# Uneven pieces of the first modulation's last block: 800 columns in six transfers in place of 480

## The chip, the cores and the metric

The kernel runs on one core of one Trainium2 chip. The metric is the device time of one execution in microseconds (us); of several runs the median is given. A profile is one execution with the hardware profiler, and its span goes from the first to the last instruction of the program.

## The reference

One token goes through an adaLN block with a cached attention and a dense layer. Cut to what matters:

```python
mod = silu(c) @ w_mod                        # c: 640, w_mod: 640 x 3840
sa, ca, ga, sb, cb, gb = six parts of 640
h = layernorm(x) * (1 + ca) + sa             # first modulation: sa, ca
q = (h @ wq)  -> 32 heads of 192
p = softmax(q . k_cache * 192**-0.5)         # k_cache, v_cache: 32 x 8192 x 192
x = x + ga * ((p . v_cache) @ wo)
h = layernorm(x) * (1 + cb) + sb
x = x + gb * (relu(h @ w1 + b1)**2 @ w2 + b2)
```

All of it is float32, and the two caches are 403 MB of the 452 MB that are read.

## The kernel before

Everything comes through one queue of transfers that SyncE (SP) issues in the order in which the code says `load`. The caches, with the slices of `wq` and `wo` that are due, lie in memory as "chunks" of 128 rows (one for each partition) of up to `SLOT` = 16128 columns. `PLAN` (from `plan`, L56) says which key positions and value units a chunk holds. Three buffers of that size (`slot`, L103) are used in turn: the weights of the first modulation take the first (`wm0_t`), chunks 0 and 1 the next two, and from there `load(n + 3)` (L435) waits until the reader of the buffer is done. After the last chunk the same queue brings the weights of the other modulations, `wm1`, and of the dense layer, `w1` and `w2`, in cuts (`WM_CUT`, `W1_CUT`, `W2_CUT`), the last of which are small: 1920, 1280 and 640 columns.

For each chunk VectorE (DVE) multiplies the keys with the query (L280) and sums over the 192 columns (L288), ScalarE (ACT) takes the exponential (L315), and TensorE (PE) multiplies the probabilities with the values (L332). The program's order on each engine is the order of the code.

The part that the change touches is the start. `mod(0, 2, wm0_t, wm0x_t)` (L252, function at L191) computes `sa` and `ca`: 640 inputs are 5 blocks of 128 (`KB` = 5), and 1280 outputs are 4 groups of 32 rows of PSUM with 2 x 160 columns each. So a block is 4 matmuls of 320 columns, with the block's `silu(c)` as the stationary operand (column b of `e`). Of the last block not all columns are loaded as a full row of each partition. The columns of `wx` (width `WX`) lie apart, in `wm0x`: the piece of each of the 128 rows goes to some partition below 64 and to one of `SX` slots there, as the table `XP` says. An entry (a, k, n) of `XP` is one transfer: k rows, at partitions a, a + 4, a + 8 and so on, with n slots each.

```python
SX = 7
XP = ((32, 8, 5), (0, 3, SX), (1, 3, SX), (2, 3, SX), (3, 3, 6), (33, 1, SX))
WX = 3 * DG
```

Here 8 x 5 + 9 x 7 + 3 x 6 + 7 = 128 pieces of 480 columns. The value of `c` that belongs to a piece lies at the same partition and slot in the columns `KB + s` of `e`, zero elsewhere, and the area of the pieces is set to zero before the transfers (L121 on DVE, L122 on GpSimd, POOL), since unused places are multiplied too. L126 issues the six transfers, right behind the main one (L123) and ahead of chunk 0 (L250). In `mod`, L205 multiplies what came as full rows, and L211 the pieces, slot by slot; it waits for all six transfers. Then come the layernorm (L158), the query of the first 512 columns (L261) and the first multiplication of keys (L280).

At the end, L475 multiplies by `w2` block by block as its cuts land, DVE makes `y` (L478, L479), and two small transfers write it out.

Of the kernel before, what the change touches and what calls it, by code (L numbers as in the profile page):

```python
# [13 lines left out]
P = 128  # L14
D = 640
# [5 lines left out]
DG = D // G  # L21
FG = FF // G
KB = DG // 32
# [13 lines left out]
UNIT = E * DH  # L37
EXTRA = {"o": WO, "q": WQ}
SLOT = 84 * DH
SX = 7  # L40
XP = ((32, 8, 5), (0, 3, SX), (1, 3, SX), (2, 3, SX), (3, 3, 6), (33, 1, SX))
WX = 3 * DG
W0 = KB * 2 * D - WX
VPC = 5
LEAD_FROM = 1300
# [41 lines left out]
def width(chunk):  # L87
    return chunk[1] * DH + chunk[3] * UNIT + sum(EXTRA[t] for t, _ in chunk[4])
# [6 lines left out]
def block_kernel(ctx: ExitStack, tc: tile.TileContext, kv, wm0, wm0x, wm1, w1, w2, out):  # L95
    nc = tc.nc
# [6 lines left out]
    def slot(name):  # L103
        return strm.tile([P, SLOT], F32, tag="slot", name=name, bufs=3)


    ident = const.tile([P, P], F32, name="ident")
    make_identity(nc, ident)
    ones = const.tile([P, P], F32, name="ones")
# [6 lines left out]
    eps_t = const.tile([P, 1], F32, name="eps_t")  # L116
    nc.gpsimd.memset(eps_t, EPS)

    wm0_t = slot("wm0_t")
    wm0x_t = wm0_t[:64, SLOT - SX * WX:]  # L120
    nc.vector.memset(wm0x_t[:, :SX // 2 * WX], 0.0)  # L121
    nc.gpsimd.memset(wm0x_t[:, SX // 2 * WX:], 0.0)  # L122
    nc.sync.dma_start(wm0_t[:, :wm0.shape[1]], wm0)  # L123
    r = 0
    for a, k, n in XP:
        nc.sync.dma_start(wm0x_t[a:a + 4 * k - 3:4, :n * WX], wm0x[r:r + k, :n * WX])  # L126
        r += k

    small = const.tile([P, 2 * KB + SX + FB + KB], F32, name="small")
    nc.vector.tensor_copy(small, wm0_t[:, W0 + WQ:wm0.shape[1]])  # L130
    x_c, c_c, bbc = small[:, :KB], small[:, KB:2 * KB + SX], small[:, 2 * KB + SX:]

# [58 lines left out]
    def mod(first, n, w, wx=None, between=lambda: None):  # L191

        ps = psum.tile([P, 512], F32, tag="q", name=f"ps_mod{first}", bufs=1)
        for b in range(KB):
            if b == 3:
                between()
            wb = w[:, b * n * D:(b + 1) * n * D]
            if wx is None or b < KB - 1:
                wb = wb.rearrange("p (m n) -> p m n", m=n)
                parts = [(g, slice(0, n * DG), wb[:, :, DG * g:DG * (g + 1)]) for g in range(G)]  # L200
            else:
                wb = wb[:, :n * 3 * DG].rearrange("p (m n) -> p m n", m=n)
                parts = [(g, slice(0, n * DG), wb[:, :, DG * g:DG * (g + 1)]) for g in range(2)] + [(2, slice(0, DG), wb[:, 0, 2 * DG:])]
            for g, at, wg in parts:
                nc.tensor.matmul(ps[32 * g:32 * (g + 1), at], e[:, b:b + 1].to_broadcast([P, 32]), wg,  # L205
                                 start=(b == 0), stop=(b == KB - 1 and (wx is None or g < 2)))
        if wx is not None:
            wx = wx.rearrange("p (s n) -> p s n", s=SX)
            for s in range(SX):
                for g, at, wg in ((2, slice(DG, 2 * DG), wx[:, s, :DG]), (3, slice(0, 2 * DG), wx[:, s, DG:])):  # L210
                    nc.tensor.matmul(ps[32 * g:32 * (g + 1), at], e[:64, KB + s:KB + s + 1].to_broadcast([64, 32]), wg,  # L211
                                     start=False, stop=(s == SX - 1))
        nc.vector.tensor_copy(mods[:, first:first + n], ps[:, :n * DG].rearrange("p (m n) -> p m n", m=n))

    def gate(m, w, steps):

        ps = psum.tile([P, 512], F32, tag="q", name=f"ps_mod{m}", bufs=1)
        b = 0
        for n in steps:
            for b in range(b, b + n):  # L220
                for k in range(2):
                    nc.tensor.matmul(ps[64 * k:64 * (k + 1), :2 * DG], e[:, b:b + 1].to_broadcast([P, 64]),
                                     w[:, b, 2 * DG * k:2 * DG * (k + 1)], start=(b == 0), stop=(b == KB - 1))
            b += 1
            yield
        for g in range(G):
            r = slice(32 * g, 32 * (g + 1))
            nc.scalar.activation(mods[r, m], ps[r, DG * (g % 2):DG * (g % 2 + 1)], AF.Copy)
        yield

    chunk_t = {}
    start = [sum(width(c) for c in PLAN[:n]) * P for n in range(len(PLAN))]
# [17 lines left out]
    load(0)  # L250
    load(1)
    mod(0, 2, wm0_t, wm0x_t)  # L252
    ma = columns(mods[:, 0:2].rearrange("p m n -> p (m n)"), 2 * DG, "ma")
    h1 = layernorm(x_c, 1, lambda: ma[:, KB:, 0], lambda: ma[:, :KB, 0], "ln1")
# [129 lines left out]
    for n, (kp, nk, vp, nv, extra) in enumerate(PLAN):  # L384
# [3 lines left out]
        at = nk * DH + nv * UNIT  # L388
# [15 lines left out]
        m = nk - FOLD * nk // 16 if kp >= FOLD_FROM else nk  # L404
# [39 lines left out]
    turn(NPAIR - 1)  # L444
    attend(*wo_t)
    mod(2, 3, wm1_t[:, KB * D:KB * 4 * D], between=gather)
    x1 = const.tile([P, DG], F32, name="x1")
    nc.vector.tensor_mul(x1, att_t[0][:, :DG], mods[:, 2])
    nc.vector.tensor_add(x1, x1, x_t)

    last = gate(5, gb_t, (2, 1, 2))
# [4 lines left out]
    for b in range(KB):  # L456
        for g in range(G):
            nc.tensor.matmul(pf[32 * g:32 * (g + 1), :FG], hT2[:, b], w1_t[:, b, FG * g:FG * (g + 1)],
                             start=(b == 0), stop=(b == KB - 1))
# [13 lines left out]
    for b in range(FB):  # L473
        for g in range(G):
            nc.tensor.matmul(py[32 * g:32 * (g + 1), :DG], fT[:, b], w2_t[:, b, DG * g:DG * (g + 1)],  # L475
                             start=(b == 0), stop=(b == FB - 1))
# [57 lines left out]
```

## Time and profile before

| | before |
|---|---|
| median of 3 runs | 1052.11 us (1052.1 to 1052.33) |
| the profiled execution | 1052.17 us |
| its span | 1050.1 us |
| DVE busy | 899.4 us (86%) |
| PE busy | 497.1 us (47%) |
| packets of the loads, share of 16 DMA engines' span | 99.4% |
| read from memory | 451.82 MB, 430 GB/s |
| instructions fetched | 16 packets of 16 KB (queue q8) |

A transfer is split into packets, and the packets run on 16 DMA engines that work side by side. A transfer of 128 rows gives 8 packets, one for each row, to each of the 16 engines; one of 8 rows gives one packet to each of 8 engines, and one of 3 rows to 3. A packet of 4 bytes after a transfer's last packet on an engine reports that its part is done. The view of DMA packets can be asked for any stretch, and it counts the packets that begin in it; the share that it prints is their whole duration over 16 times the stretch. In a stretch of 10 ns, which is 160 ns of 16 engines, a share of 788.1% is a single packet of 1.26 us. In longer stretches of equal small packets, the share times 16 is the number of engines that are at work.

### The profile page before, as it was taken

The page shows a single profiled execution, that of the slowest core. Times are in us where ns is not written, and L with a number is a line of the kernel's source. Part 1 is how long each engine was busy: PE and PEld are TensorE (multiplying, and loading weights), DVE is VectorE, ACT ScalarE, POOL GpSimd, SP SyncE. Part 2 cuts the span into 40 slices and gives each one's busy share as a digit, 9 for nine tenths or more (in the row PEclk, how much of TensorE's full clock was granted, in tenths as well). Part 3 has the DMA queues.
Part 4 walks back from the last instruction along what each step waited for, and adds up shares of the span by engine and source line. Part 5 has one row for each costly group of instructions (what it writes and reads, how often), then busy time and mean ns, then how long its engine had stood idle before and what let it go on. Part 6 is the DMA issues. An engine that isn't in the chain of part 4 may idle for free.

```text
span 1050.1 us, 4948 instructions
## 1 busy us (share of the span) xinstructions
PE 497.1 (47%) x2130; PEld 135.7 (13%) x2130; DVE 899.4 (86%) x304; ACT 51.4 (5%) x156; POOL 11.0 (1%) x12
## 2 busy tenths in 40 slices
PE   3253063655452454347354365354546346435287
PEld 1110010111010011012011011011111011001023
DVE  1699999978969989999797997999999987999822
ACT  0100000000000000000000000000000000000001
POOL 1000000000000000000000000000000000000200
PEclk9676586777666676767676577667768767668689
DMA  9999999999999999999999999999999999999998
GB/s 409 428 433 432 433 436 435 441 439 433 430 435 431 430 435 431 435 436 439 432 431 433 437 432 437 433 433 435 436 430 433 433 437 433 433 433 433 425 429 344
DMA packets 9142, 452.12 MB, mean 431 GB/s; under 512 B 1033, under 2 KB 1037, under 8 KB 1421
## 3 DMA queue, kind: packets, MB, share of 16 engines
q1 hardware_dynamic: 9118, 451.83, 99.4%
q8 instruction: 16, 0.26, 0.1%
q14 instruction: 4, 0.03, 0.0%
q10 hardware_dynamic: 4, 0.00, 0.0%
HBM read 451.82 MB, written 0.00 MB: 430 GB/s over the span
## 4 chain that ended last, share of the span: by engine, by line
DVE 51%; DMA 34%; PE 13%; ACT 1%; issue 1%; SPq 0%; DVEq 0%; ACTq 0%
DMA chunk<-in_kv 31%; DVE sc L288 24%; DVE chunk L280 24%; PE ps_o L332 7%; PE ps_q L261 2%; DMA w_t<-in_w 2%; PE att_a L361 1%; DMA wm_t<-in_wm 1%; PE ps_mx L307 1%; DVE os L345 1%; DVE ps_o L342 1%; ACT p L315 1%; DVE nm L309 1%; PE ps_mod L205 1%; DVE mp L305 0%
## 5 line engine op out<-in xcount | busy, mean ns | idle before, releaser
L280 DVE TENSOR_TENSOR chunk<-chunk,qb 128x8064 f32<-128x8064 f32 (+19 forms) x81 | 419.4, 5208 | 53.1 <-DMA chunk<-in_kv 45.9
L288 DVE TENSOR_REDUCE sc<-chunk 128x44 f32<-128x8448 f32 (+16 forms) x56 | 413.7, 7395 | 0.8
L332 PE MATMUL ps_o<-chunk,p 128*32 128x512 f32 x1536 | 295.8, 735 | 34.6 <-DMA chunk<-in_kv 25.5
L307 PE MATMUL ps_mx<-ident,mp 128*128 128x128 f32 x32 | 14.9, 464 | 352.8 <-DVE mp L305 352.8
L332 PEld LDWEIGHTS ps_o<-chunk,p 128*32 128x32 f32 x1536 | 68.0, 131 | 239.1 <-issue 196.7
L361 PE MATMUL att_a<-chunk,oW 128*32 128x512 f32 x96 | 64.7, 829 | 72.1 <-ACT oW L359 72.1
L261 PE MATMUL ps_q<-chunk,ln_h 128*128 128x512 f32 x110 | 65.6, 756 | 17.9 <-DMA chunk<-in_kv 17.8
L307 PEld LDWEIGHTS ps_mx<-ident,mp 128*128 128x128 f32 x32 | 5.7, 179 | 379.7 <-DVE mp L305 351.9
L315 ACT ACTIVATE p<-sc,nm 128x256 f32<-128x256 f32 x32 | 16.2, 508 | 622.9 <-DVE nm L309 622.9
L261 PEld LDWEIGHTS ps_q<-chunk,ln_h 128*128 128x128 f32 x110 | 26.5, 251 | 54.9 <-issue 34.4
L342 DVE TENSOR_TENSOR ps_o<-ps_o,mask 96x1024 f32<-96x1024 f32 (+1 forms) x17 | 19.7, 1156 | 8.9 <-PE ps_o L332 8.9
L361 PEld LDWEIGHTS att_a<-chunk,oW 128*32 128x32 f32 x96 | 12.2, 142 | 108.1 <-ACT oW L359 74.8
L309 DVE TENSOR_REDUCE nm<-ps_mx 128x1 f32<-128x128 f32 x32 | 9.3, 291 | 17.9 <-PE ps_mx L307 17.9
L345 DVE TENSOR_REDUCE os<-ps_o 96x128 f32<-96x1024 f32 (+1 forms) x17 | 19.7, 1158 | 0.6
L347 PE MATMUL ps_o<-ident,os 96*128 96x96 f32 x16 | 5.3, 332 | 29.0 <-DVE os L345 29.0
L409 POOL TENSOR_TENSOR chunk<-chunk 128x1824 f32<-128x1824 f32 (+1 forms) x2 | 7.9, 3940 | 980.6 <-DVE chunk L280 980.6
L320 PE MATMUL ps_sum<-ident,wide 128*128 128x128 f32 x16 | 7.6, 475 | 21.7 <-ACT wide L318 21.7
L205 PE MATMUL ps_mod<-wm_t,silu 128*32 128x480 f32 (+2 forms) x78 | 10.0, 647 | 14.5 <-DVE silu L187 14.5
L351 DVE TENSOR_REDUCE oT<-ps_o 128x3 f32<-128x96 f32 x16 | 4.0, 248 | 13.7 <-PE ps_o L347 13.7
L359 ACT ACTIVATE oW<-oT,r 128x96 f32<-128x96 f32 x16 | 5.9, 372 | 193.8 <-DVE oT L351 193.8
L363 PE MATMUL att_a<-chunk,oW 128*96 128x384 f32 x32 | 14.8, 543 | 0.0
L262 ACT ACTIVATE qb<-ps_q 128x512 f32<-128x512 f32 x12 | 7.2, 597 | 124.9 <-PE ps_q L261 124.9
(80 smaller groups left out, 103.4 us busy)
## 6 DMA issues: line engine op xcount, KB each, us to landing
chunk<-in_kv SPq DMA_DIRECT2D x38, 8064.0 KB, 31.4
chunk<-in_kv SPq DMA_DIRECT2D x11, 8000.0 KB, 33.5
chunk<-in_kv SPq DMA_DIRECT2D x2, 7872.0 KB
chunk<-in_kv SPq DMA_DIRECT2D x1, 6144.0 KB, 22.5
wm_t<-in_wm SPq DMA_DIRECT2D x1, 4480.0 KB
wm_t<-in_wm SPq DMA_DIRECT2D x1, 4257.0 KB, 12.6
chunk<-in_kv SPq DMA_DIRECT2D x1, 3264.0 KB
chunk<-in_kv SPq DMA_DIRECT2D x1, 3072.0 KB
```

Of the source, the lines that this page charges most:

```text
L205: nc.tensor.matmul(ps[32 * g:32 * (g + 1), at], e[:, b:b + 1].to_broadcast([P, 32]), wg, start=(b == 0), stop=(b == KB - 1 and (wx is None ...
L261: nc.tensor.matmul(ps, h1[:, b:b + 1].to_broadcast([P, P]), w[:, b], start=(b == 0), stop=(b == KB - 1))
L280: nc.vector.tensor_mul(pr, pr, q[:, None, :].to_broadcast([P, b - a, DH]))
L288: nc.vector.tensor_reduce(sc[:, a % SRING:a % SRING + b - a], src[:, a - first:b - first], axis=AX.X, op=ALU.add)
L307: nc.tensor.transpose(ps[:, :P], mp.to_broadcast([P, P]), ident)
L309: nc.vector.tensor_reduce(nm, ps[:, :P], axis=AX.X, op=ALU.max, negate=True)
L315: nc.scalar.activation(p, s[:, :, None].to_broadcast([P, NPOS, 32 // E]), AF.Exp, bias=nm, accum_out=sp[:, h % 2:h % 2 + 1])
L332: nc.tensor.matmul(ps_t[h // 2][32 * g:32 * (g + 1), h % 2], p[:, E * j:E * (j + 1)].rearrange("p e r -> p (e r)"), t[:, g], start=(j == 0 ...
L342: nc.vector.tensor_mul(po, po, mask[:n, None, None, :].to_broadcast([n, b - a, ED, E]))
L345: nc.vector.tensor_reduce(os_t[i][:n, a:b], po, axis=AX.X, op=ALU.add)
L361: nc.tensor.matmul(att_a[96:, :512], oW[:, j], w[:, j, :512], start=(first and j == 0), stop=(last and j == NV - 1))
L363: nc.tensor.matmul(att_a[:96, :NV * (D - 512)], oW.rearrange("p j r -> p (j r)"), w[:, :, 512:], start=first, stop=last)
```

## The change

480 of the last block's 1280 columns were pieces; now 800 are. `WX` is 800 columns, there are 5 slots instead of 7, and the table has two transfers of 8 rows with 5 slots, one of 8 rows with 2, two of 3 rows with 5, and one of a single row with 2. The full rows of `wm0` are 8192 columns wide in place of 8514. `mod` takes one matmul fewer from the full rows, and three for each of 5 slots from the pieces in place of two for each of 7. The setting to zero on DVE is moved to the front of the program and takes 3 of the 5 slots; POOL takes 2.

```diff
-SX = 7
-XP = ((32, 8, 5), (0, 3, SX), (1, 3, SX), (2, 3, SX), (3, 3, 6), (33, 1, SX))
-WX = 3 * DG
+SX = 5
+XP = ((32, 8, SX), (33, 8, SX), (34, 8, 2), (0, 3, SX), (1, 3, SX), (2, 1, 2))
+WX = 5 * DG
 W0 = KB * 2 * D - WX
...
+    wm0_t = slot("wm0_t")
+    wm0x_t = wm0_t[:64, SLOT - SX * WX:]
+    nc.vector.memset(wm0x_t[:, :3 * WX], 0.0)
     ident = const.tile([P, P], F32, name="ident")
     make_identity(nc, ident)
...
-    wm0_t = slot("wm0_t")
-    wm0x_t = wm0_t[:64, SLOT - SX * WX:]
-    nc.vector.memset(wm0x_t[:, :SX // 2 * WX], 0.0)
-    nc.gpsimd.memset(wm0x_t[:, SX // 2 * WX:], 0.0)
+    nc.gpsimd.memset(wm0x_t[:, 3 * WX:], 0.0)
     nc.sync.dma_start(wm0_t[:, :wm0.shape[1]], wm0)
...
-                wb = wb[:, :n * 3 * DG].rearrange("p (m n) -> p m n", m=n)
-                parts = [(g, slice(0, n * DG), wb[:, :, DG * g:DG * (g + 1)]) for g in range(2)] + [(2, slice(0, DG), wb[:, 0, 2 * DG:])]
+                wb = wb[:, :n * 2 * DG].rearrange("p (m n) -> p m n", m=n)
+                parts = [(0, slice(0, n * DG), wb[:, :, :DG]), (1, slice(0, DG), wb[:, 0, DG:])]
...
-                for g, at, wg in ((2, slice(DG, 2 * DG), wx[:, s, :DG]), (3, slice(0, 2 * DG), wx[:, s, DG:])):
+                for g, at, wg in ((1, slice(DG, 2 * DG), wx[:, s, :DG]), (2, slice(0, 2 * DG), wx[:, s, DG:3 * DG]),
+                                  (3, slice(0, 2 * DG), wx[:, s, 3 * DG:])):
                     nc.tensor.matmul(ps[32 * g:32 * (g + 1), at], e[:64, KB + s:KB + s + 1].to_broadcast([64, 32]), wg,
                                      start=False, stop=(s == SX - 1))
```

On SP, at the start of the program, the queue of transfers before was this; a row is line, tensor written and read, rows x columns:

```order
L123 DMA wm_t<-in_wm 128x8514
L126 DMA wm_t<-in_wm0x 8x2400
L126 DMA wm_t<-in_wm0x 3x3360 x3
L126 DMA wm_t<-in_wm0x 3x2880
L126 DMA wm_t<-in_wm0x 1x3360
L247 DMA chunk_104<-in_kv 128x12288
```

And with the change it is this:

```order
L123 DMA wm_t<-in_wm 128x8192
L126 DMA wm_t<-in_wm0x 8x4000 x2
L126 DMA wm_t<-in_wm0x 8x1600
L126 DMA wm_t<-in_wm0x 3x4000 x2
L126 DMA wm_t<-in_wm0x 1x1600
L248 DMA chunk_104<-in_kv 128x12288
```

The number of transfers stays seven ahead of chunk 0; the eight-row ones carry 9600 columns a row in place of 2400, and the three-row ones 8000 in place of 12960.

On DVE, at the start, the order before was:

```order
L113 TENSOR_REDUCE mask<-ident 128x8
L115 TENSOR_REDUCE sel<-ident 128x1
L121 MEMSET wm_t 64x1440
L130 COPY small<-wm_t 128x34
L185 TENSOR_SCALAR silu<-silu 128x12
```

And with the change:

```order
L109 MEMSET wm_t 64x2400
L116 TENSOR_REDUCE mask<-ident 128x8
L118 TENSOR_REDUCE sel<-ident 128x1
L130 COPY small<-wm_t 128x32
L185 TENSOR_SCALAR silu<-silu 128x10
```

The setting to zero moved ahead of the two small reductions, and no other instruction of DVE changed its place.

## Rows read from the trace of the kernel before

**Rows 1.** The page: span, busy times, slices of the DMA engines, queues of packets.
```profile
span 1050.1 us, 4948 instructions
...
PE 497.1 (47%) x2130; PEld 135.7 (13%) x2130; DVE 899.4 (86%) x304; ACT 51.4 (5%) x156; POOL 11.0 (1%) x12
...
DMA  9999999999999999999999999999999999999998
...
q1 hardware_dynamic: 9118, 451.83, 99.4%
q8 instruction: 16, 0.26, 0.1%
```

**Rows 2.** Chain that ended last, 0 to 120 us: start us, us, what.
```profile
0.73 12.57 DMA wm_t<-in_wm
...
14.48 5.55 PE ps_mod L205 x36
20.03 3.96 PE ps_mod L211 x21
...
36.38 12.97 DVE chunk L280
```

**Rows 3.** The same chain, 1000 us to the end.
```profile
1026.34 19.43 DMA w_t<-in_w
...
1045.80 0.75 PE ps_y L475 x16
...
1046.58 0.52 PE ps_y L475 x8
```

**Rows 4.** Stretches near the end; the last two columns: DMA share, GB/s.
```profile
1042.00:1042.90 0.90, 0.85 (x26) 0.88 (x30) 0.00 (x0) 0.00 (x0) 0.00 (x0) 1.00 1.02 427
1043.90:1045.00 1.10, 0.74 (x24) 0.68 (x24) 0.00 (x0) 0.00 (x0) 0.00 (x0) 1.00 0.74 305
1045.35:1045.60 0.25, 0.00 (x0) 0.00 (x0) 0.00 (x0) 0.00 (x0) 0.00 (x0) 1.00 0.59 236
1045.70:1045.80 0.10, 0.00 (x0) 0.00 (x0) 0.00 (x0) 0.00 (x0) 0.00 (x0) 1.00 0.52 205
1046.10:1046.20 0.10, 0.10 (x12) 0.10 (x4) 0.00 (x0) 0.00 (x0) 0.00 (x0) 1.00 0.07 25
```

**Rows 5.** DMA packets in 257.685:257.695, 260.060:260.070, 260.925:260.935 us: packets, MB, share.
```profile
q1 hardware_dynamic: 1, 0.06, 1487.5%
...
q8 instruction: 1, 0.02, 549.4%
...
q1 hardware_dynamic: 1, 0.06, 1830.6%
```

**Rows 6.** DMA packets in 12.589:12.597 us, then in 1046.100:1046.110 us.
```profile
q1 hardware_dynamic: 4, 0.02, 578.1%
...
q1 hardware_dynamic: 1, 0.00, 63.8%
```

**Rows 7.** DMA packets of 10 ns at 3.450 us, then at 38.700 us.
```profile
q1 hardware_dynamic: 1, 0.03, 788.1%
...
q1 hardware_dynamic: 1, 0.06, 1475.6%
```

**Rows 8.** Timeline, 0 to 8 us: start us, us, engine, line, instruction.
```profile
1.42 1.69 POOL L122 MEMSET wm_t<- 64x1920 f32 x1
...
1.94 1.26 DVE L121 MEMSET wm_t<- 64x1440 f32 x1 [0.24 <-issue]
...
3.29 4.10 SPq L126 DMA_DIRECT2D wm_t<-in_wm0x  x6
7.44 0.34 SPq L247 DMA_DIRECT2D chunk<-in_kv  x1
```

**Rows 9.** Timeline of SP, 60 to 66 us; then DMA packets in 64.935:64.945 us.
```profile
62.36 0.33 SPq L247 DMA_DIRECT2D chunk<-in_kv  x1
...
q1 hardware_dynamic: 3, 0.06, 1665.3%
```

More of the change, by code (lines that the diff above doesn't have):

```diff
@@ L201, in mod @@
             else:
-                wb = wb[:, :n * 3 * DG].rearrange("p (m n) -> p m n", m=n)
-                parts = [(g, slice(0, n * DG), wb[:, :, DG * g:DG * (g + 1)]) for g in range(2)] + [(2, slice(0, DG), wb[:, 0, 2 * DG:])]
+                wb = wb[:, :n * 2 * DG].rearrange("p (m n) -> p m n", m=n)
+                parts = [(0, slice(0, n * DG), wb[:, :, :DG]), (1, slice(0, DG), wb[:, 0, DG:])]
             for g, at, wg in parts:
                 nc.tensor.matmul(ps[32 * g:32 * (g + 1), at], e[:, b:b + 1].to_broadcast([P, 32]), wg,
-                                 start=(b == 0), stop=(b == KB - 1 and (wx is None or g < 2)))
+                                 start=(b == 0), stop=(b == KB - 1 and (wx is None or g < 1)))
         if wx is not None:
@@ L515 @@
     xw, cx = np.zeros((P, SX, WX), np.float32), np.zeros((P, SX), np.float32)
-    xw[xp, xs] = np.concatenate([last[:, 1, 2 * DG:3 * DG], last[:, 0, 3 * DG:], last[:, 1, 3 * DG:]], axis=1)
+    xw[xp, xs] = np.concatenate([last[:, 1, DG:2 * DG], last[:, :, 2 * DG:3 * DG].reshape(P, 2 * DG), last[:, :, 3 * DG:].reshape(P, 2 * DG)], axis=1)
     cx[xp, xs] = cc[:, KB - 1]
@@ L519 @@
         "kv": np.concatenate(kv),
-        "wm0": np.concatenate([m0[:, :(KB - 1) * 2 * D], last[:, 0, :3 * DG], last[:, 1, :2 * DG],
+        "wm0": np.concatenate([m0[:, :(KB - 1) * 2 * D], last[:, 0, :2 * DG], last[:, 1, :DG],
                                wq[0], column(A_x, KB), cc, cx, column(B_b1, FB), column(B_b2, KB)], axis=1),
```

## The prediction

> **What bounds the kernel now.** I read the page first. DVE is busy for 86% of the span, which looks like the bound, but the line of slices shows the 16 DMA engines busy from the first to the last slice, and the packets of the loads alone fill 99.4% of 16 engines' span [rows 1]. 451.83 MB over 1050.1 us at that share are 27.05 bytes per ns and engine, and a single packet has the same rate: 64000 bytes in 14.756 x 160 ns = 2361 ns, 27.1 bytes per ns [rows 7]. So each DMA engine works at a rate of its own, without a pause, from the first slice to the last. The chain ends with the transfers of `w2`, 19.43 us of them, then 0.75 and 0.52 us of PE [rows 3]: the end is set by the engine that lands its last packet last.
>
> Then I asked which engine that is. The stretches near the end show a staircase: all 16 are at work up to 1042.9 us, 0.74 x 16 = 12 up to 1045.0, 9 to 10 at 1045.5, 8 at 1045.75 and one at 1046.15 [rows 4]. The last packet begins at 1046.10 us and takes 0.638 x 160 = 102 ns [rows 6]; PE starts its last group 0.38 us later [rows 3]. So four engines finish between 1042.9 and 1043.9, two to three us early, and eight finish last, between 1045.8 and 1046.2.
>
> What makes eight engines late? The queue of instruction fetches has 16 packets [rows 1]. I followed the packets engine by engine: the next one on an engine starts within some ns of the end of the one before, and each engine has the same sequence of sizes, which keeps them apart. The 16 fetches fall on eight engines, twice on each, and these are the eight late ones. One such place: a load packet of 64512 bytes takes 14.875 x 160 = 2380 ns; the fetch after it takes 879 ns, and the load packet that follows takes 18.306 x 160 = 2929 ns (in this order in [rows 5]). So a fetch costs its engine 861 ns of gap and 549 ns of stretching, 1.41 us, and two cost 2.82 us. Without them all engines but the three with many pieces would end near 1043.
>
> **The change part by part.** It moves bytes between engines; the total stays. By engine:
>
> - Full rows: 8192 columns for 8514, on all 16 engines, 8 packets each. A packet of 34056 bytes takes 7.881 x 160 = 1261 ns [rows 7], so one of 32768 takes 1213, and each engine saves 8 x 48 = 0.38 us. No packet of 32768 bytes is in the trace; between 34056 and 64000 bytes the rates are 27.0 and 27.1, and I take 27.0.
> - Eight-row transfers: their eight engines took one packet of 9600 bytes, (578.1% x 128 ns - 2 x 9) / 2 = 361 ns by [rows 6]; those rows are two such packets, with the two of 4 bytes (9 ns each) ahead of them. Now they take 16000 + 16000 + 6400 bytes. At 27.1 bytes per ns these are 1.42 us, at the 26.6 of the 9600-byte packet 1.44, plus some 15 ns for each of the two added transfers: 1.07 to 1.11 us more. For the five of these engines that get nothing else the net is +1.09 - 0.38 = **+0.7 us** (38400 - 9600 - 10304 = 18496 bytes more).
> - Three-row and one-row transfers: these engines are three of those eight. The first had 9600 + 3 x 13440 + 11520 + 13440 = 74880 bytes in pieces and gets 76800; the other two had 61440 and get 70400. Net of the full rows that is -0.3 and about -0.05 us.
> - The other eight engines get no pieces: -0.38 us.
>
> So the sign hangs on where the fetches fall. Following the engines through, two or three of the eight that fetch are among the five. Two of them are the engines whose 9600-byte packets begin at 12.590 and 12.595 us [rows 6]; their first fetches end just before 320.13 and 260.93 us (the next packet takes 2929 ns on both; the second stands in [rows 5]), and the second is the engine that lands last of all, 495 load packets after its piece, with the packet at 1046.10 us [rows 6]. At two places an engine of the five passes within 10 ns of one of the other half, where I can't tell them apart: there one of those two, and a third engine, could be exchanged. At least one of the five remains a fetching engine, and these end at 1046.12 to 1046.20 now. They would end 0.7 us later, and the end with them: PE's last group follows the landing, and the two small transfers of the output follow PE.
>
> What lies beside this, at nothing:
>
> - PE in the modulation: 19 matmuls of L205 take 5.55 us and 14 of L211 take 3.96 [rows 2], 0.29 and 0.28 each; now 18 and 15. The pieces' matmuls have more columns (4000 for 3360), so 0 to +0.3 us. The input lands 0.38 us earlier. The first multiplication, at 36.38 us [rows 2], shifts by -0.4 to 0.
> - The pieces landing later by at most some 0.7 us: 74880 bytes at 26.6 are 2.8 us after the full rows' landing at 13.30, so 16.1 at the latest, and L211 starts at 20.03 [rows 2]. That cover is 3.9 us.
> - Setting to zero: DVE 1.26 x 2400/1440 = 2.1 us from 0.7, POOL 1.69 x 1600/1920 = 1.4 from 1.42, so done at 2.8 instead of 3.2. SP's six transfers (3.29) and chunk 0 (7.44) [rows 8] may go 0.4 us earlier. The engines are then busy with full rows until after 12 us, so it is worth nothing.
> - The cover of all these is that SP's queue never runs dry. It is thinnest at chunk 3: issued at 62.36 us when chunk 0's buffer comes free, with its first packet at 64.94, so 2.6 us ahead [rows 9]. The engines without pieces get there 0.38 us earlier, and the release moves by 0 to -0.4. It holds.
>
> Sum: the last landing moves by **+0.7 us** (0.6 if the earlier of the two engines is the one that stays). The profiled execution has 1052.17 us, 2.07 around its span, which makes 1052.87; it stands 0.06 over the median, so 1052.8 against 1052.11. 0.2% is 2.1 us, about what a measurement can tell from no change, so this counts as the same.
>
> Here a rule of the Trainium skill speaks against the mechanism. The trace has a fetch cost of 1.41 us on the engine that it hits [rows 5]. "Runtime: NRT & Kernel Launch", section "Instruction fetch mechanics", says that crossing a 16 KiB block costs one tail-bump of the DMA queue and is mostly hidden. For PE, which waits for nothing there, I see no disagreement; for the loads' engines the row says otherwise.
>
> **The rivals.**
>
> 1. *No fetching engine gets pieces.* If my following went wrong, all eight late engines lose 10304 bytes and end 0.38 us earlier, at 1045.82. The three with many pieces end by 1045.7, so they don't take over. That gives 1051.7. For it: the sets of late and early engines are certain, the link to the pieces runs through 250 to 310 us of packets. Against it: the sequences of sizes.
> 2. *The fetches don't matter to the end, and the engine with most bytes sets it.* Its pieces grow by 0.1 us and its full rows shrink by 0.38: -0.3 us, 1051.8. This is what the rule of "Runtime: NRT & Kernel Launch" in the Trainium skill would make of it. Against it: eight engines still work at 1045.75 [rows 4], and only three have many pieces.
> 3. *The queue runs dry at chunk 3, slower.* If the front were late, for instance if PE ran the modulation's 9.5 us [rows 2] at half the clock that it has there, chunk 0 would be done 9.5 us later, and the transfer into its buffer issued so much later. From a delay of at most 2.2 us on (2.6 less 0.38, and less what lies between an issue and its first packet) every us leaves all engines idle for one: at least 1052.1 + 9.5 - 2.2, about 1059.4. Nothing in PE's work ahead of the modulation changes, so I see no reason for it.
> 4. *A gain of over 2.1 us* would need fewer bytes or a faster rate; the largest gain by balance is the 1.0 us between the last landing and the mean of all engines (about 1045.2 by the staircase of [rows 4]).
>
> **How the numbers follow.** Forecast 0.78 (own range 1052.4 to 1053.1), rival 1 0.11, rival 2 0.06, rival 3 and the like 0.03, rival 4 0.02. The range takes in rivals 1 and 2, the spread of the fetch gaps and of the runs (0.2 us): 1051.6 to 1053.1. All but rivals 3 and 4 lie within 0.2%: faster 0.02, same 0.95, slower 0.03.
>
> **What would show it.** The staircase of the profile after: engines early at the end (12 at work near 1044.5) as now, but the last landing near 1046.9, with one to three engines at work alone from 1045.8 on, and the others of the late eight done by 1045.7. The packets of the full rows take 1.21 us. The first multiplication starts at 36.0 to 36.4 us. A last landing at 1045.8 means rival 1 or 2. A gap between load packets near 64.5 us, or chunk 3 issued after 63.5, means rival 3.

## The result, and the profile after

The change makes the kernel slower: 1055.69 us (median of 6 runs, 1055.46 to 1056.85) against 1052.14 (6 runs, 1051.94 to 1052.91), a ratio of 1.0034 with an interval of 1.0021 to 1.0047. I had forecast 1052.8, and slower by over 0.2% at 0.03. The profiled execution took 1055.46 us.

The page of the kernel after, its parts 1 to 3: busy times, slices, and queues (packets, MB, share of 16 engines' span).

```profile
span 1053.5 us, 4948 instructions
...
PE 487.9 (46%) x2130; PEld 133.9 (13%) x2130; DVE 900.0 (85%) x304; ACT 51.4 (5%) x156; POOL 10.7 (1%) x12
...
DMA  9999999999999999999999999999999999999997
...
q1 hardware_dynamic: 9138, 451.83, 99.4%
q8 instruction: 16, 0.26, 0.1%
```

Against [rows 1] the span is 3.4 us longer, with the same bytes, the same number of instruction fetches and the same share of 99.4%. DVE is busy for 900.0 us, where it was 899.4, and PE for 9 us less. So the DMA engines do not wait for anything new: they are as busy as before, for longer.

The chain of the kernel after, 1000 us to the end (start us, us, what):

```profile
1030.84 19.16 DMA w_t<-in_w
...
1050.04 0.52 PE ps_y L476 x8
```

The last PE group starts at 1050.04, where it was 1046.58 [rows 3]; from there to the end of the span it is 3.5 us in both. Which engines land last is seen in stretches of the kernel after near the end (stretch, its length, busy us and instructions of PE, PEld, DVE, ACT, POOL, then granted clock, DMA share, GB/s):

```profile
1046.20:1047.20 1.00, 1.00 (x32) 0.73 (x23) 0.00 (x0) 0.00 (x0) 0.00 (x0) 1.00 0.84 343
1047.20:1048.30 1.10, 0.69 (x24) 0.61 (x24) 0.00 (x0) 0.00 (x0) 0.00 (x0) 1.00 0.60 235
1048.50:1049.40 0.90, 0.34 (x12) 0.16 (x8) 0.00 (x0) 0.00 (x0) 0.00 (x0) 1.00 0.12 46
```

The form is the one that was forecast: 0.12 x 16 = 2 engines are at work alone at the end, for about 1.1 us after the third-last. But all of it stands some 2.6 us too late. 0.84 x 16 = 13 engines are still at work around 1046.7; by the forecast at most three should have been. Followed packet by packet, the two last engines land at 1049.49 and 1049.50, the next at 1048.41, and the earliest of all at 1045.1. A delay that all 16 engines share is no matter of balance.

The same place as in [rows 5], now of the kernel after: DMA packets in three stretches of 10 ns (258.757, 261.136 and 262.140 us; packets, MB, share). They are a load packet of 64512 bytes, the fetch behind it on the same engine, and the next load packet.

```profile
q1 hardware_dynamic: 1, 0.06, 1488.8%
...
q8 instruction: 1, 0.02, 636.2%
...
q1 hardware_dynamic: 1, 0.06, 1830.6%
```

The load packet takes 14.888 x 160 = 2382 ns for 2380. The fetch takes 1018 ns for 879, and the gap between the two load packets is 1000 ns for 861. On the engine that lands at 1049.50 the load packet ahead of the fetch has 1490.0%, 2384 ns. Over all 4864 packets of 64512 bytes, those with a fetch behind or beside them (above 2450 ns) left out, the mean is 2385.3 ns after and 2380.3 before; 2587 of them take 2384, 1019 take 2391. Up to some 65 us most take 2380, from there on few do. So 0.2% is lost on the packets of nearly all chunks: 5.0 ns on 28.24 MB an engine (438 packets of that size) is an estimate of 2.2 us, and two fetches of +0.14 us each make it 2.5.

What did the change do to every packet of the caches? Their bytes, sources and order are as before. Their place in memory is not. The tile `small` has 2 x 5 + `SX` + ... columns, so with `SX` from 7 to 5 it goes from 34 to 32 columns (the row of L130 in the order of DVE shows it), 136 to 128 bytes of a partition. The program hands out this memory in steps of 32 bytes, and what lies behind moves down by one step: in the program's memory map (the profile shows no addresses) the three buffers of `slot` began at byte 26368 of each partition (103 x 256), 90880 and 155392, and now begin 32 bytes lower. 64512 is 252 x 256, so before all three stood on a multiple of 256, and now none does.

### The profile page after: what moved, and what is told of

The parts are those of the page before. It is cut to its first block, busy times and chain, and to the rows that moved or that the text cites. A ratio compares the mean times of both kernels' runs of the same rounds, so it can differ in the third digit from the quotient of the medians.

```text
span 1053.5 us, 4948 instructions
## 1 busy us (share of the span) xinstructions
PE 487.9 (46%) x2130; PEld 133.9 (13%) x2130; DVE 900.0 (85%) x304; ACT 51.4 (5%) x156; POOL 10.7 (1%) x12
## 3 DMA queue, kind: packets, MB, share of 16 engines
q1 hardware_dynamic: 9138, 451.83, 99.4%
## 4 chain that ended last, share of the span: by engine, by line
DVE 51%; DMA 34%; PE 13%; ACT 1%; issue 1%; SPq 0%; DVEq 0%; ACTq 0%
DMA chunk<-in_kv 31%; DVE sc L289 24%; DVE chunk L281 24%; PE ps_o L333 6%; PE ps_q L262 2%; DMA w_t<-in_w 2%; PE att_a L362 2%; DMA wm_t<-in_wm 1%; PE ps_mx L308 1%; DVE os L346 1%; DVE ps_o L343 1%; ACT p L316 1%; DVE nm L310 1%; PE ps_mod L205 0%; DVE mp L306 0%
## 5 line engine op out<-in xcount | busy, mean ns | idle before, releaser
L333 PE MATMUL ps_o<-chunk,p 128*32 128x512 f32 x1536 | 287.6, 717 | 41.0 <-DMA chunk<-in_kv 31.9
```

Of the source, the lines that this page charges most:

```text
L333: nc.tensor.matmul(ps_t[h // 2][32 * g:32 * (g + 1), h % 2], p[:, E * j:E * (j + 1)].rearrange("p e r -> p (e r)"), t[:, g], start=(j == 0 ...
```

## The experiments

The theory was that the write address of the loads, off a multiple of 256 bytes, costs the 2.8 us, and that the balance costs the rest as forecast. Against it stood that the chip or its environment was slower at that time, that the pieces or the earlier start slow the packets down, and that any other place of the buffers costs as much. Each expectation is quoted as it stood before its run.

**The kernel before, once more.** No edit, on the chip of the runs below.

> The kernel before, unchanged, for a second trace of it. Every theory expects a time near 1052.1. What differs between the two traces of the same kernel is the environment's (theory C). Theories A and B expect load packets of 64512 bytes at 2380 ns as in the first trace, and the gap at an instruction fetch near 0.9 us. Theory C (the rate follows where the run or the tensors are placed) expects packets and gaps as in the changed kernel here: 2384 to 2391 ns and 1.0 us.

It took 1051.97 us (one run). Its load packets of 64512 bytes have a mean of 2380.2 ns and its 16 KB fetches take 879 to 968 ns, as in the first trace. So theory C falls as far as one run tells; the 21 to 33 runs of this kernel beside the runs below have medians of 1052.2 to 1052.3.

**The change, with the buffers where they were.** Two unused columns in `small`:

```diff
-    small = const.tile([P, 2 * KB + SX + FB + KB], F32, name="small")
+    small = const.tile([P, 2 * KB + SX + FB + KB + 2], F32, name="small")[:, :2 * KB + SX + FB + KB]
```

> The changed kernel with 2 unused columns behind the small tile, which puts the three chunk buffers back to byte 26368 of each partition (a multiple of 256), where the kernel before has them; the change alone moved them to 26336 (a multiple of 32 only). Theory A (the address of the buffers slows every load packet): packets back at 2380 ns, only the imbalance of +0.7 us is left, 1052.8. Theory B (the bytes per engine bring the engines into a relation in which they disturb each other) and theory C (placement): no change, 1055.7, packets at 2384 to 2391 ns.

1052.88 us (1052.74 to 1053.3, 11 runs), against 1052.22 for the kernel before: 1.0006 (0.9997 to 1.0015). The interval alone does not tell this from no difference, but all 11 runs lie above the highest of the 26 of the kernel before (1052.58). The same work, the same tensors in memory and the same pieces, 2.81 us faster than the change. The mean of the 4864 packets, the stretched ones left out as above, is 2380.2 ns again, and the fetches take 878 to 964 ns. Its stretches near the end, three of them as in [rows 4] (columns as above):

```profile
1043.90:1045.00 1.10, 0.76 (x24) 0.44 (x15) 0.00 (x0) 0.00 (x0) 0.00 (x0) 1.00 0.76 312
...
1045.70:1045.80 0.10, 0.10 (x12) 0.03 (x4) 0.00 (x0) 0.00 (x0) 0.00 (x0) 1.00 0.21 77
1045.90:1046.80 0.90, 0.38 (x15) 0.23 (x12) 0.00 (x0) 0.00 (x0) 0.00 (x0) 1.00 0.12 48
1046.80:1046.90 0.10, 0.10 (x12) 0.09 (x8) 0.00 (x0) 0.00 (x0) 0.00 (x0) 1.00 0.07 26
```

This is the forecast's staircase: 12 engines at 1044.5, three at 1045.75, two from 1045.9, and the last packet near 1046.9, where [rows 4] have 8 engines at 1045.75 and the last packet at 1046.15. The chain has PE's last group at 1047.36, 0.78 after that of [rows 3]. So the difference of +3.55 splits into 0.66 of balance and 2.81 of address, to within the spread of the medians. The last landing of the change's profiled execution comes 2.52 us after this one (1049.50 and 1046.98), which is the 2.5 estimated above; the other 0.3 us of the 2.81 is not accounted for.

**The kernel before, with its buffers moved.** 8, 16, 32 and 64 unused columns in `small`, so 32, 64, 128 and 256 bytes; the first as an example:

```diff
-    small = const.tile([P, 2 * KB + SX + FB + KB], F32, name="small")
+    small = const.tile([P, 2 * KB + SX + FB + KB + 8], F32, name="small")[:, :2 * KB + SX + FB + KB]
```

> The kernel before with 8 unused columns behind the small tile, which moves the buffers from byte 26368 to 26400 (a multiple of 32 only) and changes nothing else. Theory A: every load packet slower by 4 to 11 ns, +2.6 us, 1054.7. Theories B and C: 1052.1.

> The kernel before with 16 unused columns, buffers at byte 26432 (a multiple of 64, not of 128 or 256). Theory A with a step of 64 bytes: 1052.1, as before. Theory A with a step of 128 or 256 bytes: 1054.7. Theories B and C: 1052.1.

> The kernel before with 32 unused columns behind the small tile: buffers at byte 26496 of a partition, a multiple of 128 and not of 256. Offsets of 32 and 64 cost 2.7 and 2.2 us. If the step is 256 bytes, about +2 us, 1054.2; if it is 128, 1052.2 as before.

> The kernel before with 64 unused columns: buffers at byte 26624, again a multiple of 256, and all small tiles behind the first one moved too. If the address of the buffers within 256 bytes is the cause, 1052.2 and load packets at 2380 ns. If it was the moving of the small tiles, or of the buffers by any amount, 1054 or more.

| bytes | median us (range) | median before, same chip | ratio (interval) | mean packet ns |
|---|---|---|---|---|
| +32 | 1054.90 (1054.61 to 1055.93) | 1052.22 | 1.0027 (1.0018 to 1.0036) | 2385.2 |
| +64 | 1054.42 (1054.26 to 1055.38) | 1052.22 | 1.0022 (1.0013 to 1.0031) | 2383.7 |
| +128 | 1054.24 (1054.07 to 1055.33) | 1052.28 | 1.0019 (1.0010 to 1.0028) | 2383.7 |
| +256 | 1052.23 (1051.94 to 1052.69) | 1052.28 | 1.0000 (0.9991 to 1.0009) | 2380.2 |

Nothing of the change is in these kernels, and the first has the change's loss without its pieces. That another place as such costs nothing is shown by +256. The step is 256 bytes, and not 32, 64 or 128. Single stretches of 1 us that hold only packets of 64512 bytes say the same; the share times 16000 ns, divided by the packets, is their mean. The kernel before at 306.850, packets, MB, share:

```profile
q1 hardware_dynamic: 11, 0.71, 163.6%
```

The kernel with 128 bytes more, at the same time:

```profile
q1 hardware_dynamic: 12, 0.77, 178.9%
```

The change itself, at 307.050, and the change with the buffers where they were, at 306.650:

```profile
q1 hardware_dynamic: 10, 0.65, 149.0%
...
q1 hardware_dynamic: 10, 0.65, 148.8%
```

These are 2380, 2385, 2384 and 2381 ns.

**One buffer of three aligned.** Is it the address that a packet writes, or a state that all packets share? In the kernel before, each buffer is made 8 columns longer, so the first stays on a multiple of 256 and the others are off by 32 and by 64:

```diff
-        return strm.tile([P, SLOT], F32, tag="slot", name=name, bufs=3)
+        return strm.tile([P, SLOT + 8], F32, tag="slot", name=name, bufs=3)[:, :SLOT]
```

> The kernel before with 8 unused columns behind each of the three buffers: the first (chunks 2, 5, 8 and so on) stays at a multiple of 256 bytes, the second (chunks 1, 4, 7) lies 32 and the third (chunks 0, 3, 6) 64 bytes past one. If a load packet is slowed by the address that it is written to, the packets of chunks 5, 8 and so on stay at 2380 ns while their neighbours in time, which are written to the other two, take 2382 to 2391 ns; the time is +(0 + 2.7 + 2.2)/3 = +1.6 us, 1053.9. If it is the engines' reading of the buffers or a state of the whole transport, all chunks are slowed alike, 1054.4 or more.

1053.69 us (1053.32 to 1054.4) against 1052.27, 1.0014 (1.0006 to 1.0023). Two stretches of 1 us of this kernel, both of 64512-byte packets: at 496.850 us, chunk 25 into the buffer that is 32 off, and at 515.900, chunk 26 into the aligned one.

```profile
q1 hardware_dynamic: 11, 0.71, 164.2%
...
q1 hardware_dynamic: 11, 0.71, 163.6%
```

2388 and 2380 ns, 19 us apart: chunks that follow each other in time differ by the buffer that they are written to. From chunk 13 (258 us) on, the packets of chunks 13, 16, 19 and so on have a mean of 2385.3 ns, those in the aligned buffer 2380.9. The first take mostly 2384 and 2391 ns, as do the packets of the kernel with 32 bytes more; with 64 more they take mostly 2382 and 2389.

Two things do not fit a cost of the packet's own write address alone. The chunks of the other unaligned buffer have a mean of 2380.8 ns, no more than the aligned ones, though the whole kernel at 64 bytes off lost 2.2 us. And from 262 us on all fetches take 1016 to 1100 ns, those beside chunks of the aligned buffer too (1062 ns at 687 us, 1089 at 967). So some of it is a state that packets share. What makes an offset cost here and not there, and from another time on in each run, is open.

That the time came near the 1053.9 expected is in part luck. The third buffer's share of that sum is missing; in its place, the load packets of 64512 bytes that begin between 63.5 and 67 us, where chunk 3 starts, are longer than 2380 ns by 6.1 us in all, 0.38 us an engine. In the first trace of the kernel before it is 1.1 us in all.

**Other balances.** With the alignment kept, three tables spread the pieces otherwise. The first two change the table alone, in the kernel of the second experiment; six rows for each of the first six engines:

```diff
-XP = ((32, 8, SX), (33, 8, SX), (34, 8, 2), (0, 3, SX), (1, 3, SX), (2, 1, 2))
+XP = ((32, 6, SX), (33, 6, SX), (34, 6, SX), (35, 6, SX), (0, 6, 1), (1, 2, 1))
```

> The changed kernel with the buffers back at byte 26368, and the 128 pieces of 800 columns in four transfers of 6 rows with 5 slots, one of 6 with 1 and one of 2 with 1, so that six DMA engines get 64000 to 70400 bytes each and the other ten none. By the balance theory the two fetching engines of the eight-row group lose 38400 bytes or 1.42 us, so they no longer end alone behind all others; the other fetching engines end at 1045.7; what decides is whether the engine that takes two of the smaller 8 KB fetches is among the six: then it ends near 1046.7 and the time is 1052.8, else 1051.8. If instead the pieces' engines don't matter, 1052.9 as with eight rows and with no change of the order in which engines end.

1053.99 us (1053.72 to 1054.62), 1.0016 (1.0007 to 1.0025) against 1052.28. A miss: one of these six engines does have two fetches of 16 KB (at 65 and 612 us), and its 67200 bytes of pieces make it the last by 1 us. The expectation had put no engine with fetches of 16 KB among the six. Two stretches of this kernel, columns as above:

```profile
1045.90:1046.80 0.90, 0.90 (x24) 0.67 (x24) 0.00 (x0) 0.00 (x0) 0.00 (x0) 1.00 0.11 46
1046.90:1047.80 0.90, 0.38 (x14) 0.36 (x16) 0.00 (x0) 0.00 (x0) 0.00 (x0) 1.00 0.06 23
```

Two engines (0.11 x 16), then one. The last lands at 1047.84; the other, which has two fetches of 8 KB (a second, smaller kind), at 1046.85. The other fetching engines, without pieces, land between 1045.4 and 1045.8, and 67200 bytes at 27.1 bytes per ns are 2.5 us: the sum of pieces and fetches sets the end, engine by engine.

Then all 16 engines alike, so that the eight fetching ones get as many bytes as the others:

```diff
-XP = ((32, 8, SX), (33, 8, SX), (34, 8, 2), (0, 3, SX), (1, 3, SX), (2, 1, 2))
+XP = ((0, 16, SX), (1, 16, 3))
```

> The changed kernel with the buffers back at byte 26368, and the pieces in two transfers of 16 rows (5 and 3 slots), so that all 16 engines get 25600 bytes each and the imbalance of the bytes is gone; only that of the fetches is left. By the balance theory all eight fetching engines carry 15296 bytes more than the six of them without pieces did before, 0.56 us, and end near 1046.6: +0.4 us on the kernel before, 1052.6. If evenly spread bytes are what counts, faster than before, 1051.8.

1053.60 us (1053.35 to 1054.04), 1.0013 (1.0004 to 1.0022) against 1052.28. Slower, as the balance says, but by 1 us more than its sum. One cause stands at the start. DMA packets of this kernel in 13.135:13.140 and 13.140:13.150 us (packets, MB, share):

```profile
q1 hardware_dynamic: 1, 0.02, 1468.8%
...
q1 hardware_dynamic: 1, 0.05, 1612.5%
```

A piece of 16000 bytes takes 14.688 x 80 = 1175 ns, and a chunk's packet of 49152 bytes next to it 2580. In the kernel with eight-row transfers every such piece takes 596 ns (372.5% of 160 at 11.870 us), and the packets of 49152 bytes 1815. While 16 engines write rows that lie at every fourth partition from 0 to 61, pieces and the packets beside them are slowed: the 16 pieces of 16000 bytes take 596 to 1175 ns, 757 on average, those of 9600 bytes 683 where [rows 6] have 361, and the first packets of 49152 bytes 2264. Over these rates, an engine's two pieces and its chunk packets of 49152 bytes take 0.16, 0.32 and 0.45 us longer, together 0.93, an estimate that covers the 1 us. The end of this kernel in one stretch:

```profile
1046.70:1047.60 0.90, 0.36 (x12) 0.35 (x16) 0.00 (x0) 0.00 (x0) 0.00 (x0) 1.00 0.40 157
```

The eight engines with fetches of 16 KB land between 1047.2 and 1047.7, together; the others were done by 1045.0, but for one with two fetches of 8 KB, at 1046.9.

Last, the kernel before with 640 columns as pieces, in transfers of 5, 5, 4, 4, 3 and 1 rows, so that the engines with fetches of 16 KB get none (the lines that give `mod` and the inputs the new widths are left out):

```diff
-XP = ((32, 8, 5), (0, 3, SX), (1, 3, SX), (2, 3, SX), (3, 3, 6), (33, 1, SX))
-WX = 3 * DG
+XP = ((32, 5, SX), (33, 5, SX), (34, 4, SX), (35, 4, 3), (0, 3, 4), (1, 1, 6))
+WX = 4 * DG
...
```

> A version after the balance theory: 640 columns as pieces (full rows of 8354 columns), 34, 28, 28, 24 and 14 of the 128 pieces to the first five DMA engines and none to the others, buffers at a multiple of 256 bytes. By the ends of the engines in the trace of the kernel before: the fetching engines without pieces lose 0.19 us, 1045.9; the two of the old eight-row group lose 0.54, 1045.7; the first three engines end near 1045.9, 1045.9 and 1045.5. If the engine with the two smaller fetches is the fifth, it ends at 1045.8, and the last landing is 1045.9: -0.3 us, 1052.0. If it is the fourth, it ends at 1046.8 and the time is 1052.8. If a fetching engine is among the five, it ends at 1047.1 or later, 1053.1.

1052.63 us (1052.37 to 1052.84) against 1052.27, 1.0003 (0.9994 to 1.0012): no difference that can be measured. Its last stretches:

```profile
1046.60:1046.70 0.10, 0.10 (x11) 0.10 (x4) 0.00 (x0) 0.00 (x0) 0.00 (x0) 1.00 0.06 25
1046.70:1046.80 0.10, 0.10 (x12) 0.00 (x0) 0.00 (x0) 0.00 (x0) 0.00 (x0) 1.00 0.01 0
```

One packet begins after 1046.6, that of an engine with two fetches of 8 KB and 61440 bytes of pieces, so the fourth of the five. It lands at 1046.71: of the cases expected this is the second, 1046.8 and 1052.8. But a fetching engine without any piece lands at 1046.57, later than the last of the kernel before (1046.20) and 0.7 us later than expected; why is open. No table that was run beats the kernel before; whether another would is not shown.

## Why the prediction was wrong

- **The step that failed** is the first of the change, "It moves bytes between engines; the total stays", with the rate for the packets: 27.1 bytes per ns was taken for all loads after the change because it was that of all loads before. The change moves no byte of the caches, but shrinks a tile ahead of their buffers by 8 bytes, and with the addresses moves the rate: 2385 for 2380 ns a packet, and a gap of 1000 for 861 ns at the fetch of [rows 5]. This is a cost of 2.81 us (the change against its aligned version), which neither the sum nor a rival held. Rival 3, the one on the slower side, looked for idle engines, and none idled.
- Could the trace of before have shown it? The rate no, since every chunk lay on a multiple of 256 there. The shift yes: the order of DVE, which the prediction read for the setting to zero alone, has the copy of 34 columns become 32.
- **Balance: right.** +0.7 was forecast, and +0.66 measured with the alignment restored, the last landing 0.78 later; two engines are alone at the end, landing at 1046.88 and 1046.98 for the forecast 1046.9. Both have 38400 bytes of pieces and two fetches (at 261 and 813 us, and at 320 and 891). The following of engines through 300 us of packets held, so rivals 1 and 2 fall. The full rows take 1213 ns for a forecast of 1213 (758.1% of 160 at 11.535 us, kernel after).
- **Fetches: right, but one kind was left out.** Gap and stretching together are 1.41 to 1.42 us at every fetch of 16 KB that was followed in the kernel before and in the aligned change, and 1.55 to 1.56 in the change. In the six-row kernel the engine with both fetches and pieces lands last by 1 us. The page of the kernel before has a second queue of fetches, of which the prediction says nothing:

```profile
q14 instruction: 4, 0.03, 0.0%
```

These four of 8 KB cost their engine 0.55 to 0.84 us each in that trace. Two fall on one engine, which lands at 1045.03, 1.9 us after one with the same bytes and no fetch; so not all engines but the three with many pieces and the eight with fetches of 16 KB would end near 1043. In the aligned change this engine lands at 1045.80, third from the end, and does not set the time.
- **Rival 2's rule** would have gained 0.3 us (1051.8). That was not seen with the alignment restored, where two fetching engines with pieces land 1 us after all others. The rule is that of "Runtime: NRT & Kernel Launch" in the Trainium skill, section "Instruction fetch mechanics" (mostly hidden); the 1.41 us above do not agree with it for this kernel's loads.
- **The front: wrong, without effect.** The first multiplication was to start at 36.0 to 36.4 us. The chain of the kernel after, 0 to 120 us (start us, us, what), has it earlier:

```profile
14.26 4.91 PE ps_mod L205 x35
19.17 2.84 PE ps_mod L212 x21
...
34.53 12.97 DVE chunk L281
```

The multiplication of the pieces takes 2.84 us for 3.96 [rows 2] at the same granted clock of 1.00, though it has 4000 columns for 3360. It is 2.84 in all four kernels with the change's matmuls, and 3.90 to 4.14 in all others. Before, its matmuls alternated between two groups of PSUM rows, now they go over three. The number of columns does not explain it: the last kernel of the experiments has 14 matmuls over the same two groups as before with 4480 columns, and they take 3.91 us. The groups were not changed alone, so that they are the cause is not shown.

The rest of the shift is no more than the spread between executions. The second trace of the unchanged kernel has its first multiplication at 34.98 us and issues chunk 3 at 60.95, where the first has 36.38 and 62.36 [rows 9] and the change 34.53 and 60.50. Those two executions of the same kernel took 1051.97 and 1052.17 us. So 1.4 us here go with 0.2 us of the time, which is within the spread of the runs, and this fits what the prediction said of anything that comes earlier in the front.

## What to carry to other kernels

In this kernel, which its loads bound, the address of a load's buffer is part of its cost: all buffers 32, 64 or 128 bytes off a multiple of 256 made packets of 64512 bytes up to 11 ns longer, and the kernel 0.2 to 0.3% slower. Before costing an edit, list every tile whose size it changes and see what lies behind it in memory, and pin the large buffers (a padded width, or allocating them first) before comparing versions, or a change of 0.06% is measured as one of 0.34%. And balance load engines by the time each one ends, with the instruction fetches it serves counted in, not by bytes. Even so such a sum missed here where it did not know which engine would fetch (six rows) and where the pieces themselves became slower (sixteen).

## What the runs showed of the hardware

- **The write address, modulo 256 bytes.** Lost in us: 2.81 at 224 off (the change), 2.7 at 32, 2.2 at 64, 2.0 at 128, nothing at 256. The Trainium skill, "DMA: Bandwidth & Descriptors", section "How a descriptor splits into AXI transactions", states that a transfer is cut into pieces of 256 bytes from aligned addresses, and that a start off them costs beats of 32 bytes. The step of 256 agrees with the runs. The sizes do not: by the page 32 off would cost one beat in 2016, an estimate of 1.2 ns, and 128 off four times as much, where the means show 4.9 and 3.4 ns; and the page speaks of reads, while here the written address alone moved. With one buffer of three aligned, one of the two others cost nothing, so the offset is not the whole condition.
- **Fetches slow down with it.** In the kernel after, the fetch of [rows 5] takes 1018 ns for 879, and all 16 have a mean of 1064 for 928. It goes with the buffers' address: 929 in the aligned change and with 256 bytes more, 1063, 1053 and 1059 with 32, 64 and 128. The fetches' own address was not varied, and no experiment tells how the buffers come to matter to them.
- **It is not there from the start.** Most packets are at 2380 ns up to 65 us in the change and 84 us with 32 bytes, half or more of them up to about 220 us with 64 and 128, and most up to 258 us with one buffer aligned. This is open as well.
- **Many single rows at once.** 16 engines that write single rows to partitions 0 to 61 together take 596 to 1175 ns for 16000 bytes, where eight of them take 596. It was seen in one kernel, at one place, and nothing there tells the partitions apart from the number of engines.
